# The first pair of tanh rows of the first chunk: by TensorE transposes and VectorE copies, or by a transposing transfer

## Chip, cores and metric

The kernel runs on one core of one Trainium2 chip. The metric is the device time of one execution in microseconds; several runs are made and their median is given. The engines are TensorE (PE, with PEld for its weight loads), VectorE (DVE), ScalarE (ACT), GpSimd (POOL) and SyncE (SP), which only issues transfers.

## The reference

A speech encoder's joint network with its gradients, forward and backward in one program, all in bf16. x is [2, 16000, 256]. Two convolutions over time (3 taps, stride 2, each followed by a gelu) make f of [2, 4000, 256], and then:

```
fe = f @ w_f                                  # [b, t, 256]
ge = g @ w_g                                  # [b, 8, 256]
j  = tanh(fe[:, :, None, :] + ge[:, None, :, :])   # [2, 4000, 8, 256]
out = j @ w_o                                 # [2, 4000, 8, 256]
```

Given grad_out of out's shape, it also returns the gradients of x, w1, w2, g, w_f, w_g and w_o. The one that the change touches is the gradient of w_o: the sum over b, t and u of j (as a column) times grad_out (as a row).

## The kernel before

The two sequences of 4000 steps of t are laid end to end (with 16 columns between them) and cut into 16 chunks of 512 columns (`CW`, the last of 336). In a chunk everything stands with the 256 features on partitions (two tiles of 128, `KT`) and time along the free dimension. The 8 values of u are taken in 4 pairs (`up`), two u each.

One pair of a chunk runs through these steps (`joint_units`):

- `tanh` (L415): ScalarE writes JT, the tanh of FE plus a bias from GE, four instructions of 128x512 for a pair.
- `gj` (L659), for each u: ScalarE squares JT into JSQ; TensorE multiplies grad_out's columns (GOT) with w_o (L672); VectorE makes NGZ from JSQ and that product (L676). Four NGZ for a pair. GpSimd adds the NGZ up (L696).
- `o_block` (L717): the output rows, 4 blocks of 128 time steps, matmuls with JT as the weights (L722), then a copy out of PSUM to OUT (L724). In the first chunk blocks 1 and 3 are copied by VectorE, the others by ScalarE.
- `gwo` (L753): the gradient of w_o, 16 matmuls per pair that add into one PSUM tile, GWO_ps (L761). It contracts over time, so it needs the tanh rows with time on partitions: JR, the transposed JT, and GO, grad_out's rows. `gwo` of a pair runs inside the next pair's `joint_units` (`prev_gwo`).

JR is made by `load_jr` (L698): one transposing transfer from SBUF to SBUF, issued on SyncE's queue (L703), for a whole pair: 128 partitions x 2048 values. It is called right behind the pair's `tanh`.

SyncE's queue issues in order. Besides JR it carries the transposing loads of grad_out (GOT, L174, three buffers) and of x (XC, L162), the plain loads of grad_out's rows (GO, L204, three buffers), and the rows of F (FR, L506).

All matmul results but GWO_ps go through one pool of 7 PSUM tiles (`ps_f32` and `ps_bf`, one tag). So a new matmul group can start when an earlier tile has been copied out. The transposes by TensorE that the kernel has already (`transposes`, L492, and the weights' at L845) use the same pool, an identity matrix as the second operand, and a copy out by VectorE or ScalarE (L498, L846).

Between a pair's steps, `weave` (L774) puts work of other chunks: after each step of the pair it advances a list of units (`parts`) by a ratio, 0.4 in the first chunk. In the first chunk (n = 0, the `else` at L880) there is no backward work of an earlier chunk; the list holds empty units, the second convolution of the next chunk (`conv2`, L370) and its FE (L394). `weave` also issues the gelu steps that were put off (`later`, `late`; L277, L282).

The order of instructions on each engine is made by the framework's scheduler from these calls, so it follows the code only roughly; semaphores are set by it as well.

Of the kernel before, what the change touches and what calls it, by code (L numbers as in the profile page):

```python
# [13 lines left out]
BF16 = mybir.dt.bfloat16  # L14
# [8 lines left out]
P = 128  # L23
KT = 2
# [8 lines left out]
def kernel(  # L33
# [22 lines left out]
    nc = tc.nc  # L56
# [7 lines left out]
    def geom(n):  # L64
        c0 = n * CW
        return c0, min(CW, L - c0)
# [23 lines left out]
    def blocks(w):  # L90
        return [(o, min(P, w - o)) for o in range(0, w, P)]
# [29 lines left out]
    jrp = pool("jrp", 3)  # L121
# [5 lines left out]
    def ps_f32():  # L127
        return psp.tile([P, 512], FP32, name="ps", tag="ps")

    def ps_bf():  # L130
        return psp.tile([P, 8, P], BF16, name="pst", tag="ps")


    ident = const.tile([P, P], BF16, name="ident")
# [16 lines left out]
    S = [dict() for _ in range(G)]  # L151
# [122 lines left out]
    def pump(k):  # L274
        for _ in range(k):
            if later:
                later.popleft()()  # L277
# [107 lines left out]
    def fe_units(n):  # L385
        c0, W = geom(n)
        if n > 0:
            pump(len(later))
        FE = fep.tile([P, KT, CW], FP32, name="FE")
        S[n]["FE"] = FE  # L390
        for mt in range(KT):
            ps = ps_f32()
            for kt in range(KT):
                nc.tensor.matmul(ps[:, :W], lhsT=WF[:, kt, mt * P:(mt + 1) * P], rhs=S[n]["FT"][:, kt, :W],  # L394
                                 start=(kt == 0), stop=(kt == KT - 1))
            nc.scalar.copy(out=FE[:, mt, :W], in_=ps[:, :W])
            yield
# [7 lines left out]
    def packed(ap, names, n, **kw):  # L405

        W = geom(n)[1]
        nb = -(-W // P)
        if nb * P == CW:
            return ap  # L410
        flat = ap.rearrange(f"p {names} -> p ({names})")
        size = flat.shape[1] // (CW // P) * nb
        return flat[:, :size].rearrange(f"p ({names}) -> p {names}", **kw)
# [245 lines left out]
    def gj(n, u):  # L659
        c0, W = geom(n)  # L660
        st = S[n]
        JT, GOT = st["JT", u], st["GOT", u]
        JSQ = jsp.tile([P, KT, CW], BF16, name="JSQ")
        jsq = nc.scalar.activation(out=JSQ[:, :, :W], in_=JT[:, :, :W], func=ACT.Square)  # L664
        if u == U - 4:
            st["JSQ"] = jsq
        NGZ = ngzp.tile([P, KT, CW], BF16, name="NGZ")
        st["NGZ", u] = NGZ
        for mt in range(KT):
            ps = ps_f32()  # L670
            for kt in range(KT):
                nc.tensor.matmul(ps[:, :W], lhsT=WOT[:, kt, mt * P:(mt + 1) * P], rhs=GOT[:, kt, :W],  # L672
                                 start=(kt == 0), stop=(kt == KT - 1))
            for b, lo, hi in spans(n):
                slot = n if b == 0 else n - segs_b1
                nc.vector.scalar_tensor_tensor(out=NGZ[:, mt, lo:hi], in0=JSQ[:, mt, lo:hi], scalar=1.0, in1=ps[:, lo:hi],  # L676
                                               op0=ALU.subtract, op1=ALU.mult,
                                               accum_out=NGGEc[:, b, mt, u, slot:slot + 1])
            yield
# [18 lines left out]
    def load_jr(n, up):  # L698

        W = geom(n)[1]  # L700
        JR = packed(jrp.tile([P, 2, KT, 4, P], BF16, name="JR")[:], "u k a d", n, u=2, k=KT, d=P)
        S[n]["JR", up] = JR
        S[n]["JRD", up] = nc.sync.dma_start_transpose(out=JR.rearrange("p u k a d -> p (u k a) d"),  # L703
                                    in_=S[n]["JTP", up].rearrange("p u k w -> p (u k w)"))

    def joint_units(n, up):
        c0, W = geom(n)
        st = S[n]
        bl = blocks(W)
        us = (2 * up, 2 * up + 1)  # L710
        for u in us:
            yield from gj(n, u)
            ngfe_acc(n, u)
        OUT = outp.tile([P, 4, 2 * V], BF16, name="OUT")
        JR = st["JR", up]

        def o_block(k):  # L717
            o, M = bl[k]
            ps = ps_f32()
            for j, u in enumerate(us):  # L720
                for kt in range(KT):
                    nc.tensor.matmul(ps[:M, j * V:(j + 1) * V], lhsT=st["JT", u][:, kt, o:o + M], rhs=WO[:, kt, :],  # L722
                                     start=(kt == 0), stop=(kt == KT - 1))
            (nc.vector.tensor_copy if n == 0 and k % 2 else nc.scalar.copy)(out=OUT[:M, k, :], in_=ps[:M, :])  # L724

        pend = prev_gwo[0]
        o_block(0)
        yield
        o_block(1)
        yield  # L730
        if pend is not None:
            gwo(*pend, 0)
        yield
        if pend is not None:
            gwo(*pend, 1)
        yield
        for k in range(2, len(bl)):
            o_block(k)
            yield
            if pend is not None:  # L740
                gwo(*pend, k)
        yield
        if pend is not None:
            for k in range(len(bl), len(blocks(geom(pend[0])[1]))):
                gwo(*pend, k)
        yield
        prev_gwo[0] = (n, up)
        for b, q, m, p0, p1, k, nb in joint_rows(n):
            nc.gpsimd.dma_start(out=joint_dram(out_0, b, q, m, up, nb), in_=OUT[p0:p1, k:k + nb, :])  # L749
# [3 lines left out]
    def gwo(n, up, k):  # L753
        bl = blocks(geom(n)[1])
        if k >= len(bl):
            return
        o, M = bl[k]
        JR, GO = S[n]["JR", up], S[n]["GO", up]
        for j in range(2):
            for dt in range(KT):  # L760
                nc.tensor.matmul(GWO_ps[:, dt, :], lhsT=JR[:M, j, dt, k, :], rhs=GO[:M, k, j * V:(j + 1) * V],  # L761
                                 start=(n_gwo[0] == 0), stop=(n_gwo[0] == last_gwo))
                n_gwo[0] += 1
# [6 lines left out]
    def empty(k):  # L770
        for _ in range(k):
            yield
# [88 lines left out]
        pass  # L861
    for u in range(2):
        tanh(0, u)
    load_jr(0, 0)

    for n in range(G):
        back, fwd = n > 0, n + 1 < G
        conv = conv_units(n + 1) if back and fwd else iter(())
        conv2 = conv2_units(n + 1) if fwd else iter(())
        late_open[0] = False  # L870
        parts = []
        if back:
            d1, e, rows, ghr = d1_units(n - 1), e_units(n - 1), row_units(n - 1), ghr_units(n - 1)
            parts += [islice(conv, 2), islice(d1, 1), islice(conv, 1), d1, conv, braid(rows, d5_units(n - 1)),
                      gwf_units(n - 1), gw2_units(n - 1), islice(ghr, 1), islice(conv2, 1), ghr, conv2, islice(e, 6)]
            if fwd:
                parts.append(fe_units(n + 1))
            parts.append(e)
        else:
            parts += [empty(6), islice(conv2, 1), empty(3), conv2, empty(6), fe_units(n + 1)]  # L880
        if not fwd:
            parts.insert(0, empty(2))
        fill = chain(*parts)
        ratio = (0.92 if n > 0 else 0.4) if n + 1 < G else 0.72
        for up in range(U // 2):
            step = n * (U // 2) + up
            if step + 2 < len(orderp):
                load_got(*orderp[step + 2])
            if step + 1 < len(orderp):
                load_go(*orderp[step + 1])  # L890
            if up == 3:
                load_fr(n)
            if back and up < 2 and n < G - 1:
                load_xr(n - 1, 2 * up)
                load_xr(n - 1, 2 * up + 1)
            if n == G - 2 and up >= 2:
                for piece in ((0,), (1, 2))[up - 2]:
                    load_xr_early(n, piece)
            main = joint_units(n, up)
            weave(main, fill, ratio)  # L900
            if up == U // 2 - 1:
                for _ in fill:
                    pump(2)
                    pump_late(1)
                pump(len(later))
                late_open[0] = True
                pump_late(len(late))
            for i in range(2):
                if 2 * step + 2 + i < len(order):
                    tanh(*order[2 * step + 2 + i])  # L910
            if step + 1 < len(orderp):
                load_jr(*orderp[step + 1])
            if n + 2 < G:
                load_x(n + 2, (((0,), (1,), (), ()) if n == 0 else ((), (0,), (1,), ()))[up])
    n = G - 1
# [75 lines left out]
```

## Time and profile before

| what | value |
|---|---|
| median of 3 runs | 826.83 us (825.32 to 827.06) |
| the profiled execution, its own time | 818.44 us |
| span of its instructions | 816.4 us |
| TensorE busy, matmuls | 794.3 us (97%) |
| VectorE busy | 624.7 us (77%) |
| ScalarE busy | 673.1 us (82%) |
| JR transfers | 64, landing 4.4 to 17.0 us after issue, median 8.8 |

Times in the profile count from the span's start. `L761` is line 761 of the kernel. A row of the timeline gives start, length, engine, line, operation, tiles as out<-in, and how many instructions were merged; in brackets stands how long the engine was idle before and what ended that. PE's rows overlap, since a matmul's start comes before the end of the one ahead of it. The granted clock is TensorE's, 1.00 being full speed.

### The profile page before, as it was taken

Reading aid. Unit: us, or ns where it says so; the run is one execution under the profiler, and the core shown is the slowest. Engines: PE = TensorE matmul, PEld = TensorE weight load, DVE = VectorE, ACT = ScalarE, POOL = GpSimd, SP = SyncE. Lnnn points to the kernel's source line nnn. Section 1 sums busy time; section 2 is a strip of 40 time slices with the busy share of each in tenths; the row PEclk is TensorE's granted clock in tenths of the full one; section 3 lists DMA queues with packets and bytes.
Section 4 is the critical chain, followed back from the end, with each engine's and each line's share of the span. In section 5 each row is a group of like instructions: output and inputs, shape, how many; then the busy total and the mean of one; then the engine's idle time right before and its main releaser. Section 6 shows DMA issues by size and latency. Waiting matters only on the chain.

```text
span 816.4 us, 16454 instructions
## 1 busy us (share of the span) xinstructions
PE 794.3 (97%) x6233; PEld 592.8 (73%) x6310; DVE 624.7 (77%) x1199; ACT 673.1 (82%) x1068; POOL 392.0 (48%) x418
## 2 busy tenths in 40 slices
PE   8788999999999999999999999999999999999998
PEld 3455877867777776777768778687786777778796
DVE  4988786977869778697886868778697786968744
ACT  5888897996979979799797978969799697987743
POOL 1364454553454535445476634535445355445641
PEclk9999999999999999999999999999999999999999
DMA  9999999999999999999999999999999999999954
GB/s 220 205 248 259 231 274 151 248 228 225 233 265 235 273 241 264 172 259 179 265 187 264 250 235 227 264 217 267 239 211 270 231 235 243 257 205 295 259 109 140
DMA packets 401423, 189.38 MB, mean 232 GB/s; under 512 B 349296, under 2 KB 385048, under 8 KB 401344
## 3 DMA queue, kind: packets, MB, share of 16 engines
q1 hardware_dynamic: 381104, 121.43, 83.0%
q0 software_dynamic: 20240, 66.89, 26.1%
q8 instruction: 49, 0.80, 0.4%
q14 instruction: 30, 0.25, 0.1%
HBM read 51.39 MB, written 50.34 MB: 125 GB/s over the span
## 4 chain that ended last, share of the span: by engine, by line
PE 86%; ACT 5%; DVE 4%; DMA 3%; issue 1%; POOL 0%; SPq 0%
PE GWO_ps L761 13%; PE ps L722 12%; PE ps L672 11%; PE ps L627 10%; PE ps L640 10%; PE ps L337 8%; PE ps L564 5%; PE pst L496 5%; PE ps L370 4%; PE ps L483 4%; PE ps L546 2%; DMA JR<-JT 2%; PE ps L460 1%; ACT JT L423 1%; PE ps L394 1%
## 5 line engine op out<-in xcount | busy, mean ns | idle before, releaser
L696 POOL TENSOR_TENSOR ACCN<-ACCN,NGZ 128x1024 f32<-128x1024 f32 (+1 forms) x80 | 168.3, 2104 | 69.2 <-DVE NGZ L676 68.4
L676 DVE SCALAR_TENSOR_TENSOR NGZ<-JSQ,ps 128x512 bf16<-128x512 bf16 (+3 forms) x272 | 168.2, 639 | 41.2 <-PE ps L672 33.3
L423 ACT ACTIVATE JT<-FE,GE 128x512 bf16<-128x512 f32 (+3 forms) x272 | 176.2, 711 | 0.5
L724 ACT CAST OUT<-ps 128x512 bf16<-128x512 f32 (+1 forms) x244 | 141.9, 596 | 32.0 <-PE ps L722 31.8
L664 ACT ACTIVATE JSQ<-JT 128x1024 bf16<-128x1024 bf16 (+1 forms) x128 | 135.1, 1058 | 35.8 <-DVE NGZ L676 35.6
L761 PE MATMUL GWO_ps<-GO,JR 128*128 128x256 bf16 (+1 forms) x1008 | 149.2, 274 | 5.8 <-DMA JR<-JT 4.8
L722 PE MATMUL ps<-WO,JT 128*128 128x256 bf16 (+1 forms) x1008 | 147.9, 273 | 0.1
L749 POOL DMA_DIRECT2D out_dram<-OUT x76 | 55.8, 734 | 170.1 <-ACT OUT L724 156.2
L672 PE MATMUL ps<-GOT,WOT 128*128 128x512 bf16 (+1 forms) x481 | 133.5, 376 | 1.4 <-DVE W2T L846 1.0
L761 PEld LDWEIGHTS <-JR 128*128 128x128 bf16 (+1 forms) x1008 | 97.4, 98 | 33.5 <-DMA JR<-JT 6.0
L722 PEld LDWEIGHTS <-JT 128*128 128x128 bf16 (+1 forms) x1008 | 97.5, 98 | 21.4 <-ACT JT L423 0.4
L627 PE MATMUL ps<-W1T,GH 128*128 128x256 bf16 (+2 forms) x756 | 100.2, 273 | 0.7
L277 DVE SCALAR_TENSOR_TENSOR g_s<-g_sq,g_x 128x1024 bf16<-128x1024 bf16 (+2 forms) x35 | 69.4, 1982 | 31.5 <-ACT g_sq L277 31.5
L627 PEld LDWEIGHTS <-GH 128*128 128x128 bf16 (+2 forms) x756 | 83.5, 116 | 13.0
L337 PE MATMUL ps<-XC,W 128*128 128x512 bf16 (+1 forms) x358 | 85.2, 374 | 3.0 <-DVE NGZ L676 1.8
L640 PE MATMUL ps<-rows,XR 128*128 128x256 bf16 (+1 forms) x708 | 84.7, 273 | 0.0
L630 ACT CAST GX<-ps 128x512 bf16<-128x512 f32 (+2 forms) x126 | 72.4, 589 | 12.1 <-PE ps L627 6.9
L444 DVE TENSOR_TENSOR ACC<-ACC,ps 128x512 f32<-128x512 f32 x84 | 57.5, 684 | 31.2 <-PE ps L564 24.8
L259 POOL DMA_DIRECT2D out_dram<-GX x66 | 36.2, 549 | 88.0 <-ACT GX L630 86.4
L640 PEld LDWEIGHTS <-XR 128*128 128x128 bf16 (+1 forms) x708 | 69.3, 98 | 11.0
L672 PEld LDWEIGHTS <-WOT 128*128 128x128 bf16 x512 | 48.4, 98 | 32.9 <-issue 2.4
L337 PEld LDWEIGHTS <-W 128*128 128x128 bf16 x384 | 37.4, 98 | 40.5 <-issue 3.0
(134 smaller groups left out, 1214.8 us busy)
## 6 DMA issues: line engine op xcount, KB each, us to landing
GO<-in_grad_out_dram SPq DMA_DIRECT2D x56, 512.0 KB, 5.8
out_dram<-OUT POOLq DMA_DIRECT2D x56, 512.0 KB, 6.1
out_dram<-GX POOLq DMA_DIRECT2D x55, 256.0 KB, 5.0
XR<-in_x_dram POOLq DMA_DIRECT2D x36, 256.0 KB, 6.8
XR<-in_x_dram POOLq DMA_DIRECT2D x12, 320.0 KB, 7.9
GO<-in_grad_out_dram SPq DMA_DIRECT2D x4, 384.0 KB, 5.9
out_dram<-OUT POOLq DMA_DIRECT2D x4, 384.0 KB, 5.6
GOT<-in_grad_out_dram SPq DMA_TRANSPOSE x68, 6.8
```

Source lines behind the costliest of these rows:

```text
L337: nc.tensor.matmul(ps[:, :W], lhsT=W1[:, i, kt, mt * P:(mt + 1) * P], rhs=st["X", c][:, kt, 16 + sh:16 + sh + W], start=(k == 0), stop=(k ...
L423: act = nc.scalar.activation(out=JT[:, mt, lo:hi], in_=S[n]["FE"][:, mt, lo:hi], func=ACT.Tanh, bias=GE[:, b, mt, u:u + 1], scale=1.0)
L627: nc.tensor.matmul(ps[:M, cj * D:(cj + 1) * D], lhsT=GH[:, par, kt, o:o + s * (M - 1) + 1:s], rhs=W1T[:, i, kt, :], start=(j == 0), stop=( ...
L630: nc.scalar.copy(out=t[:M, 2 * cp:2 * cp + 2, :], in_=ps[:M, :])
L640: nc.tensor.matmul(ps[:, dt * D:(dt + 1) * D], lhsT=x_row(4 * k + i + 2 * (1 - par))[:M, dt * P:(dt + 1) * P], rhs=t[:M, g + 2 * par:g + 2 ...
L664: jsq = nc.scalar.activation(out=JSQ[:, :, :W], in_=JT[:, :, :W], func=ACT.Square)
L672: nc.tensor.matmul(ps[:, :W], lhsT=WOT[:, kt, mt * P:(mt + 1) * P], rhs=GOT[:, kt, :W], start=(kt == 0), stop=(kt == KT - 1))
L676: nc.vector.scalar_tensor_tensor(out=NGZ[:, mt, lo:hi], in0=JSQ[:, mt, lo:hi], scalar=1.0, in1=ps[:, lo:hi], op0=ALU.subtract, op1=ALU.mul ...
L696: st["last"] = engine.tensor_tensor(out=out, in0=in0, in1=st["NGZ", u][:, :, :W], op=ALU.add)
L722: nc.tensor.matmul(ps[:M, j * V:(j + 1) * V], lhsT=st["JT", u][:, kt, o:o + M], rhs=WO[:, kt, :], start=(kt == 0), stop=(kt == KT - 1))
L724: (nc.vector.tensor_copy if n == 0 and k % 2 else nc.scalar.copy)(out=OUT[:M, k, :], in_=ps[:M, :])
L761: nc.tensor.matmul(GWO_ps[:, dt, :], lhsT=JR[:M, j, dt, k, :], rhs=GO[:M, k, j * V:(j + 1) * V], start=(n_gwo[0] == 0), stop=(n_gwo[0] == ...
```

## The change

Pair 0 of chunk 0 no longer calls `load_jr`. A generator, `turned_jr`, makes its JR instead: for each of the two u of the pair one PSUM tile, 8 transposes of 128x128 on TensorE into it, and one copy of 128x1024 into JR by VectorE. The generator is put at the head of the first chunk's list of fill units, where its two units take the place of two of the six empty ones. So it runs inside `joint_units` of pair 0, its first unit after about three steps of the pair and its second after about five. JR is used first in pair 1, by `gwo`. The other 63 pairs keep the transfer.

```
+    def turned_jr(n, up):
+
+        JR = jrp.tile([P, 2, KT, 4, P], BF16, name="JR")
+        S[n]["JR", up] = JR
+        for j in range(2):
+            ps = ps_bf()
+            for i in range(KT * 4):
+                nc.tensor.transpose(out=ps[:, i, :], in_=S[n]["JT", 2 * up + j][:, i // 4, i % 4 * P:(i % 4 + 1) * P],
+                                    identity=ident[:])
+            nc.vector.tensor_copy(out=JR[:, j].rearrange("p k a d -> p (k a) d"), in_=ps[:])
+            yield
+
     def joint_units(n, up):
...
-        JR = st["JR", up]
...
-    load_jr(0, 0)
+    turned0 = turned_jr(0, 0)
...
-            parts += [empty(6), islice(conv2, 1), empty(3), conv2, empty(6), fe_units(n + 1)]
+            parts += [turned0, empty(4), islice(conv2, 1), empty(3), conv2, empty(6), fe_units(n + 1)]
```

The line `JR = st["JR", up]` in `joint_units` was not used there.

## The prediction

> **What bounds the kernel now.** I read the page first: who is busy, and which chain of work ended last.
>
> ```profile
> span 816.4 us, 16454 instructions
> PE 794.3 (97%) x6233; PEld 592.8 (73%) x6310; DVE 624.7 (77%) x1199; ACT 673.1 (82%) x1068; POOL 392.0 (48%) x418
> PE 86%; ACT 5%; DVE 4%; DMA 3%; issue 1%; POOL 0%; SPq 0%
> ```
>
> TensorE (PE) works 794.3 of 816.4 us, so only its 22 us of idle time can be won. The table by stretches shows how little of that the change can reach.
>
> ```profile
> 32.40:35.40 3.00, 0.01 (x1) 0.00 (x0) 3.00 (x8) 3.00 (x5) 0.00 (x0) 1.00 0.99 222
> 35.40:39.70 4.30, 4.27 (x20) 2.61 (x21) 4.25 (x12) 2.57 (x4) 4.14 (x4) 0.60 0.59 132
> 39.70:45.80 6.10, 5.96 (x39) 3.56 (x38) 3.10 (x8) 4.90 (x8) 4.39 (x3) 1.00 1.13 307
> 45.80:47.60 1.80, 0.00 (x0) 0.00 (x1) 1.61 (x5) 1.80 (x4) 0.15 (x1) 1.00 1.14 378
> 47.60:55.00 7.40, 7.26 (x52) 4.92 (x53) 6.17 (x12) 6.03 (x9) 5.21 (x3) 1.00 1.08 167
> 55.00:70.00 15.00, 12.94 (x77) 7.34 (x77) 14.96 (x28) 12.86 (x21) 9.65 (x8) 1.00 1.10 271
> 100.00:800.00 700.00, 695.06 (x5541) 528.01 (x5609) 541.84 (x1024) 588.14 (x938) 348.54 (x367) 1.00 1.12 235
> ```
>
> The columns are the stretch, its length, busy us of PE, PEld, DVE, ACT, POOL, then the granted PE clock and the DMA share. From 100 to 800 us PE works 695.06 of 700: a head start gained before 100 us reaches the end, because nothing behind it has slack to absorb it. Three things matter before that: PE stands still for 3.00 us at 32.4; the clock is 0.60 in the 4.30 us behind that; PE stands still again for 1.80 us at 45.8. Note that VectorE (DVE) is full (3.00 of 3.00, 4.25 of 4.30) exactly where the change adds work to it.
>
> The chain that ended last names both holes, and the timeline of PE the first:
>
> ```profile
> 29.63 5.75 DMA JR<-JT
> 35.43 0.43 PE GWO_ps L761 x2
> 36.71 0.21 PE GWO_ps L761
> 36.92 0.85 PE ps L672 x2
> 37.77 2.12 PE GWO_ps L761 x13
> 39.89 0.49 PE ps L722 x5
> 40.38 7.17 DMA JR<-JT
> 47.60 1.05 PE GWO_ps L761 x8
> 48.65 1.32 PE ps L370 x6
> ```
>
> ```profile
> 31.39 1.03 PE L672 MATMUL ps<-GOT,WOT 128*128 128x512 bf16 x3
> 35.43 0.43 PE L761 MATMUL GWO_ps<-GO,JR 128*128 128x256 bf16 x2 [3.02 <-DMA JR<-JT]
> ```
>
> The first chunk's first JR (pair 0), issued at 29.63, lands 5.75 us later, and PE waits 3.02 us for it. That is the transfer the change removes. The second JR (pair 1) is issued at 40.38, lands 7.17 us later, and PE waits for it again. The order on an engine is not that of the code: pair 0's GWO_ps matmuls ran before pair 1's output matmuls (L722), which the code writes first. So the place of the new instructions is an assumption.
>
> **The transfer that goes.** The order of SyncE's queue:
>
> ```profile
> 29.63 4.00 SPq L703 DMA_TRANSPOSE JR<-JT  x1
> 33.73 5.38 SPq L174 DMA_TRANSPOSE GOT<-in_grad_out_dram  x2
> 39.92 0.37 SPq L204 DMA_DIRECT2D GO<-in_grad_out_dram  x1
> 40.38 4.61 SPq L703 DMA_TRANSPOSE JR<-JT  x1
> ```
>
> Issuing JR 0 holds the queue 4.00 us. Without it the two GOT transfers behind it may start up to 4 us sooner; the second still waits until pair 1's L672 matmuls have read its buffer. PE waited for no GOT in this stage, so I count their head start at nothing by itself. GO at 39.92 takes the buffer of GO 0, free only when pair 0's GWO_ps matmuls end (39.89 in the chain), and JR 1 at 40.38 queues right behind it. So the end of pair 0's GWO_ps matmuls sets when JR 1 starts, 0.49 us later.
>
> **The transposes that come.** Sixteen, in two groups of 8. The nearest rows are the weights' transposes of the same size, and the rows' transposes with their copy of 128x1024 out of PSUM:
>
> ```profile
> 23.21 0.83 PE L845 MATMUL pst<-ident,W 128*128 128x128 bf16 x12
> 71.82 0.68 DVE L498 COPY rows<-pst 128x1024 bf16<-128x1024 bf16 x1
> 72.42 0.69 DVE L277 TENSOR_TENSOR HT<-g_s,g_x 128x1024 bf16<-128x1024 bf16 x1
> ```
>
> Twelve take 0.83 us; with the last one's drain of 0.22 taken off, they are 0.055 us apart. 16 x 0.055 = 0.9 us of PE, which lies in the 3.02 us hole: 0 on the path. If that cover were gone, 0.9. One copy occupies VectorE for 0.60 us (71.82 to 72.42), two for 1.2, and VectorE has no gap there. Each group also takes one of the 7 PSUM tiles that all stages share until its copy is done. PE gets such tiles as VectorE and ScalarE empty them, so pair 0's later matmuls (output blocks, L722) may come some 0.5 us later, and ScalarE's copies of them with it. ScalarE has room for that:
>
> ```profile
> 40.36 0.58 ACT L724 CAST OUT<-ps 128x512 bf16<-128x512 f32 x1 [2.39 <-PE ps L722]
> ```
>
> It idles 2.39 us before this, so 0. The new waits: a group of transposes waits for its PSUM tile, and behind it on PE stand pair 0's last L672 and L722 matmuls; a copy waits for its transposes, and behind it on VectorE stand the fourth NGZ and HT, and behind those ScalarE's next squares. Transposes at 29 to 31 us are done before VectorE gets to the copies, so I count no wait there.
>
> **When JR 0 is ready now.** This decides, and it is read from VectorE's own order:
>
> ```profile
> 33.03 1.21 DVE L277 SCALAR_TENSOR_TENSOR g_s<-g_sq,g_x 128x1024 bf16<-128x1024 bf16 x1
> 34.17 0.68 DVE L277 TENSOR_TENSOR HT<-g_s,g_x 128x1024 bf16<-128x1024 bf16 x1
> 34.77 0.67 DVE L676 SCALAR_TENSOR_TENSOR NGZ<-JSQ,ps 128x512 bf16<-128x512 bf16 x1
> 35.50 0.69 DVE L277 TENSOR_TENSOR HT<-g_s,g_x 128x1024 bf16<-128x1024 bf16 x1
> 36.11 1.28 DVE L724 CAST OUT<-ps 128x512 bf16<-128x512 f32 x2
> 37.31 0.68 DVE L676 SCALAR_TENSOR_TENSOR NGZ<-JSQ,ps 128x512 bf16<-128x512 bf16 x1
> 39.13 0.68 DVE L676 SCALAR_TENSOR_TENSOR NGZ<-JSQ,ps 128x512 bf16<-128x512 bf16 x1
> 40.80 0.69 DVE L724 CAST OUT<-ps 128x512 bf16<-128x512 f32 x1 [0.98 <-PE ps L722]
> ```
>
> In the code the first copy comes behind pair 0's third NGZ (done at 33.03 here), the second behind pair 0's first output block, that is ahead of the two OUT copies at 36.11. With the first copy anywhere before 34.77, the fourth NGZ ends at 35.38 + 0.60 = 35.98, HT at about 36.6, and the second copy at about 37.2. The bounds: 34.2, if both copies directly follow the third NGZ (33.03 + 1.2); 38.4, if the second falls behind both OUT copies (37.2 + 1.2). I take 37.2, the code's order.
>
> So JR 0 comes later than before (37.2 against 35.38), and still I expect a gain, because of what PE does meanwhile. Before, half of pair 1's L672 matmuls stood behind the first two GWO_ps matmuls and ran after the hole, at the lowered clock. Now I expect them in the hole, (each 0.43 us of PE for its pair, as fast as VectorE frees PSUM tiles at 33.03 and 33.6: the last ends near 34.3), and the hole then runs only from about 34.3 to 37.2 and is followed by 16 GWO_ps matmuls alone. At full clock (1.05 us for 8 with a drain: 0.11 apart) they take 16 x 0.109 = 1.74 us and end at 37.24 + 1.74 = 38.98, where they ended at 39.89: **-0.9 us**.
>
> **The second term.** JR 1 is then issued at 38.98 + 0.49 = 39.47. Its 7.17 us had GO, the second GOT and an OUT store for company; JR 0 needed 5.75. Two transposing transfers are further ahead now, so I take 6.1, between them and nearer 5.75, and land JR 1 at 45.57 instead of 47.55: -2.0 together, **-1.1 us** of it from the landing. PE itself arrives at 38.98 + 5.9 = 44.9, so JR 1 is still last. Bounds of this term: 0 (7.17 stays) and -1.4 (5.75).
>
> Behind it, L370 at 48.65 feeds ScalarE and the VectorE stretch from 55 to 70, full with 14.96 of 15.00 and so moved as a whole. Sum: -2.0 us, from 818.44 us of the profiled execution (span 816.4 and 2.04 around it) to 816.4. The median of the runs shown, 826.83, lies 8.39 above that execution; I carry the difference over: **824.8 us**.
>
> **The rivals.** *A, VectorE takes it back* (no change). The 1.2 us delays everything on it behind the copies: the last NGZ ends at 40.95 instead of 39.74, and its next OUT copy, which came at 40.80 after a wait of 0.98, then cannot come before 40.95. If the chain behind runs over VectorE rather than over JR 1, the sum is +0.15 us: 827.0. For it: VectorE is full from 32.4 to 39.7 us and again from 55 to 70. Against: it is busy only 3.10 of 6.10 us from 39.7 to 45.8, so it can catch up before JR 1 lands.
>
> *B, the copy stands too far back and the clock falls* (slower). Place: the second copy behind the two OUT copies, done at 38.4. PE then idles from 34.3 to 38.4, 4.1 us. The hole of 3.02 us cost the clock (0.60 behind it: a GWO_ps matmul every 0.21 us instead of 0.11), the one of 1.80 did not (1.00). So the price is 16 x 0.21 = 3.4 us, the matmuls end at 41.8, and with JR 1's 7.17 unchanged the chain is +1.9: 828.7. It decides from a second copy ending at 36.5 on: at half clock that gives 39.9, as before. If the clock fell at my 37.2, the matmuls would end at 40.6, and with 6.1 for JR 1 the sum is -0.4, no change.
>
> The Trainium skill, "TensorE: Matmul & The Clock Gate" ("Why this matters for your kernels"), says that idle gaps of more than about 3 us put the clock back to half, and Part 4 that transposes do not count as busy for this gate. The first agrees with the two holes here; of the second no run here shows anything, and by it the transposes at the hole's edge would lengthen it for the gate and make B's price due in my own case.
>
> ```profile
> 35.37 0.71 ACT L423 ACTIVATE JT<-FE,GE 128x512 bf16<-128x512 f32 x1
> ```
>
> *C, JR 1 gets ahead in SyncE's queue* (faster still). If JR 1 is placed ahead of GO, it starts when pair 1's last tanh is done (36.1 before, 36.5 to 36.7 behind the first copy) and lands before PE gets there, even after 7.17 us: 43.9 at most. PE then starts JR 1's matmuls at 44.9 instead of 47.60: -2.7, 815.7, or 824.1 on the median. For it: the order is made anew. Against: before, JR 1 was placed behind GO. The most that can be won is both holes and the slow clock: 3.02 + 1.80 + (4.30 - 2.6, which is 16 x 0.109 + 4 x 0.21) less 0.9 for the transposes, 5.6 us: 821.2.
>
> That the change doesn't do what it says (the transfer still there, or the fill shifted) I see no room for: two fill units replace two of six empty ones.
>
> **How the numbers follow.** Forecast 33%, C 12%, A 30% (with the half clock at 37.2), B 25%. A measurement of this kernel can tell about 0.2%, 1.65 us. Faster by more: forecast and C, 45%. Within: A, 30%. Slower: B, 25%. The likeliest time is 824.8; its own range with C is 821.8 to 825.2. The range for 8 in 10 takes in most of B: 821.8 to 829.4.
>
> **What would show it.** Right: PE no longer waits for a JR transfer at 32 to 35 us; the second copy of JR 0 ends near 37.2, PE idles under 3 us before, the clock of the next 4 us is 1.00; the last GWO_ps matmul of pair 0 ends near 39.0; JR 1 is issued near 39.5 and lands near 45.6; from 100 us on everything is about 2 us earlier. Wrong: a clock well under 1 between 36 and 42 us and JR 1 issued after 41 (B); JR 1 lands sooner but VectorE's stretch from 55 to 70 starts where it did (A); JR 1 issued ahead of GO (C). My sum falls if the new order moves pair 1's output matmuls ahead of pair 0's GWO_ps matmuls.

## The result and the profile after

In one comparison of 22 runs each, the changed kernel took a median of 822.47 us (817.38 to 847.04) and the kernel before 826.32 us (819.11 to 840.12): 3.85 us less. The medians here and below are over all runs, while the ratios leave out the slow ones, which lie over 1.5% above the fastest run of the same kernel. The ratio is 0.9941, with a 95% interval of 0.9913 to 0.9969: 0.59% faster. The forecast was -2.0 us, or 0.24%. The profiled execution of the changed kernel took 817.38 us, with a span of 815.6 us. That is only 1.06 us less than the profiled execution of before (818.44). So most of the gain isn't in the two traces that one would lay side by side first. Executions of one and the same kernel scatter by 10 us and more in most sets of runs.

The page of the changed kernel, its totals and its chain of work:

```profile
span 815.6 us, 16487 instructions
PE 793.9 (97%) x6248; PEld 593.4 (73%) x6326; DVE 625.8 (77%) x1201; ACT 673.0 (83%) x1068; POOL 392.7 (48%) x418
PE 85%; ACT 4%; DMA 4%; DVE 4%; issue 1%; POOL 1%; SPq 0%; POOLq 0%; DVEq 0%
```

The same stretches as before (PE, PEld, DVE, ACT, POOL busy, then the granted clock, the DMA share and GB/s):

```profile
32.40:35.40 3.00, 1.78 (x8) 0.77 (x8) 3.00 (x7) 3.00 (x5) 0.00 (x0) 1.00 1.21 242
35.40:39.70 4.30, 3.27 (x22) 2.24 (x23) 4.30 (x10) 4.30 (x7) 2.98 (x3) 1.00 0.77 153
39.70:45.80 6.10, 6.10 (x45) 4.30 (x44) 6.02 (x17) 5.64 (x9) 5.98 (x5) 1.00 1.15 119
45.80:47.60 1.80, 1.75 (x12) 1.06 (x11) 0.00 (x0) 0.00 (x0) 1.72 (x2) 1.00 1.08 353
47.60:55.00 7.40, 6.02 (x46) 4.20 (x45) 7.30 (x12) 6.10 (x9) 2.85 (x2) 1.00 1.16 285
55.00:70.00 15.00, 10.97 (x59) 5.79 (x60) 15.00 (x28) 11.49 (x18) 8.68 (x8) 1.00 1.13 253
100.00:800.00 700.00, 695.18 (x5543) 528.19 (x5610) 541.74 (x1024) 588.14 (x938) 348.55 (x367) 1.00 1.10 235
```

The first hole of before is filled in part and the second whole (PE 1.78 of 3.00 in the place of 0.01, 1.75 of 1.80 in the place of 0.00), and in this execution the clock is 1.00 throughout. But PE has lost time in the last two stretches of the start: 6.02 of 7.40 in the place of 7.26, 10.97 of 15.00 in the place of 12.94. VectorE is full there. From 100 to 800 us nothing differs.

The timeline of PE shows what came in the place of the holes, and those of VectorE and ScalarE where the copies went and what they waited for:

```profile
29.52 0.61 PE L713 MATMUL pst<-ident,JT 128*128 128x128 bf16 x8
35.81 0.59 PE L672 MATMUL ps<-GOT,WOT 128*128 128x512 bf16 x2 [0.90 <-DVE JR L715]
36.24 0.38 PE L772 MATMUL GWO_ps<-GO,JR 128*128 128x256 bf16 x2
41.76 0.60 PE L772 MATMUL GWO_ps<-GO,JR 128*128 128x256 bf16 x4
44.79 1.04 PE L772 MATMUL GWO_ps<-GO,JR 128*128 128x256 bf16 x8
51.92 1.08 PE L733 MATMUL ps<-WO,JT 128*128 128x256 bf16 x8 [1.31 <-ACT g_x L373]
53.07 1.05 PE L772 MATMUL GWO_ps<-GO,JR 128*128 128x256 bf16 x8
58.91 1.02 PE L394 MATMUL ps<-FT,WF 128*128 128x512 bf16 x3 [3.05 <-DVE FT L277]
```

```profile
35.08 0.68 DVE L715 COPY JR<-pst 128x1024 bf16<-128x1024 bf16 x1
36.88 0.68 DVE L715 COPY JR<-pst 128x1024 bf16<-128x1024 bf16 x1
47.70 0.69 DVE L735 CAST OUT<-ps 128x512 bf16<-128x512 f32 x1 [1.98 <-DMA out_dram<-OUT]
56.86 2.00 DVE L277 TENSOR_TENSOR FT<-g_s,g_x 128x1024 bf16<-128x1024 bf16 x1
```

```profile
47.69 0.58 ACT L735 CAST OUT<-ps 128x512 bf16<-128x512 f32 x1 [2.34 <-DMA out_dram<-OUT]
51.30 0.57 ACT L373 CAST g_x<-ps 128x512 bf16<-128x512 f32 x1
```

SyncE's queue has another order than before:

```profile
31.34 3.06 SPq L174 DMA_TRANSPOSE GOT<-in_grad_out_dram  x1
36.47 1.77 SPq L703 DMA_TRANSPOSE JR<-JT  x1
38.29 3.89 SPq L162 DMA_TRANSPOSE XC<-in_x_dram  x1
42.28 5.20 SPq L174 DMA_TRANSPOSE GOT<-in_grad_out_dram  x1
47.57 3.02 SPq L703 DMA_TRANSPOSE JR<-JT  x1
```

JR 1 is issued at 36.47 us (40.38 before), ahead of the second GOT and of GO (50.69 us), which used to stand in front of it. Its matmuls start at 44.79 us in the place of 47.60, without a wait. That is rival C of the prediction. By pair 2 (53.07 against 54.44) half of these 2.81 us is gone, and when PE starts the GWO_ps matmuls of chunk 1's second pair (96.50 against 96.77) only 0.28 us is left. That last start is the measure used below: from there on these two executions run at a constant distance (0.28 us again at 396 and at 745 us), and others do unless a later stall disturbs them. The rest of the 0.8 us between the two spans comes behind 745 us.

### The profile page after: what moved, and what is told of

The parts are those of the page before. It is cut to its first block, busy times and chain, and to the rows that moved or that the text cites. A ratio compares the mean times of both kernels' runs of the same rounds, so it can differ in the third digit from the quotient of the medians.

```text
span 815.6 us, 16487 instructions
## 1 busy us (share of the span) xinstructions
PE 793.9 (97%) x6248; PEld 593.4 (73%) x6326; DVE 625.8 (77%) x1201; ACT 673.0 (83%) x1068; POOL 392.7 (48%) x418
## 4 chain that ended last, share of the span: by engine, by line
PE 85%; ACT 4%; DMA 4%; DVE 4%; issue 1%; POOL 1%; SPq 0%; POOLq 0%; DVEq 0%
PE GWO_ps L772 12%; PE ps L733 12%; PE ps L672 10%; PE ps L627 10%; PE ps L640 10%; PE ps L337 8%; PE pst L496 5%; PE ps L564 5%; PE ps L483 5%; PE ps L370 4%; PE ps L546 2%; ACT JT L423 2%; PE ps L460 1%; DMA XR<-in_x_dram 1%; PE ps L394 1%
## 5 line engine op out<-in xcount | busy, mean ns | idle before, releaser
L733 PE MATMUL ps<-WO,JT 128*128 128x256 bf16 (+1 forms) x1008 | 148.4, 272 | 2.6 <-ACT g_x L373 1.3
L733 PEld LDWEIGHTS <-JT 128*128 128x128 bf16 (+1 forms) x1008 | 97.5, 98 | 24.2 <-issue 3.2
L277 DVE SCALAR_TENSOR_TENSOR g_s<-g_sq,g_x 128x1024 bf16<-128x1024 bf16 (+2 forms) x35 | 67.5, 1930 | 32.0 <-ACT g_sq L277 32.0
```

## The experiments

Two questions: why did the 2.8 us not stay in the profiled executions, and where is the larger gain of the medians? Each run below is set against runs of the kernel before on the same chip. "Start" is the time at which PE starts the GWO_ps matmuls of chunk 1's second pair.

| kernel | median us (runs) | ratio to before | span us | JR 1's matmuls | start | VectorE idle 30 to 70 us |
|---|---|---|---|---|---|---|
| before | 826.32 (22) | | 816.4 | 47.60 | 96.77 | 4.51 |
| before_third | 825.98 (6) | 1.0015 [0.9973, 1.0057] | 819.1 | 48.43 | 97.65 | 4.77 |
| before_again | 825.19 (12) | 1.0009 [0.9972, 1.0046] | 821.0 | 49.72 | 101.49 | 7.17 |
| before_light | 824.48 (12) | 0.9988 [0.9955, 1.0020] | 822.5 | 51.31 | 102.92 | 10.53 |
| before_warm | 828.72 (12) | 1.0018 [0.9974, 1.0061] | 828.9 | 52.96 | 99.76 | 4.12 |
| before_warm2 | 823.16 (12) | 0.9967 [0.9928, 1.0007] | 825.6 | 52.65 | 99.45 | 4.69 |
| after | 822.47 (22) | 0.9941 [0.9913, 0.9969] | 815.6 | 44.79 | 96.50 | 1.98 |
| after_again | 821.24 (12) | 0.9957 [0.9911, 1.0004] | 817.0 | 44.75 | 97.79 | 2.62 |
| after_light | 818.78 (12) | 0.9958 [0.9924, 0.9993] | 827.2 | 45.90 | 98.61 | 2.29 |
| kept_transfer | 821.66 (12) | 0.9965 [0.9927, 1.0002] | 817.2 | 45.22 | 96.92 | 2.62 |
| order_only | 820.23 (12) | 0.9975 [0.9936, 1.0014] | 817.4 | 46.97 | 98.05 | 4.18 |
| order_again | 820.64 (6) | 0.9954 [0.9907, 1.0000] | 836.8 | 46.50 | 97.57 | 3.51 |
| late_jr1 | 820.79 (12) | 0.9967 [0.9930, 1.0005] | 825.2 | 49.72 | 96.41 | 0.03 |
| late_again | 820.19 (6) | 0.9944 [0.9900, 0.9988] | 819.5 | 50.73 | 97.51 | 0.03 |
| two_pairs | 819.24 (12) | 0.9964 [0.9933, 0.9995] | 818.0 | 46.36 | 97.30 | 0.03 |
| two_again | 823.42 (6) | 0.9962 [0.9906, 1.0018] | 831.1 | 46.32 | 97.27 | 0.03 |

The spans over 823 us hold stalls behind 340 us, told of below; their starts come before these.

### The changed kernel and the one before, once more

The same two kernels, unedited, under new names.

after_again: 

> The changed kernel, unaltered, run again beside the kernel before, to see what repeats. Theory Q (SyncE's queue): the second JR is issued ahead of GO and the second GOT, so pair 1's GWO_ps matmuls start near 44.8 us (before: 47.6), and the 0.6% seen over 22 runs is the price of the stages in front of 100 us in an ordinary execution: ratio 0.991 to 0.997. Theory C (chance): the two profiled executions differ by 0.8 us of span only, and the 0.6% comes from how the executions fell: ratio 0.998 to 1.002.

before_again: 

> The kernel before, unaltered, as a control against itself. In four kernels that differ from it only in the first 60 us, about half of the runs lay within 2 us of their fastest, and of its own runs 7 in 57. Theory B (before is really hit more often by late stalls): ratio 0.998 to 1.002 and again few runs within 2 us of the fastest. Theory M (what is run as the reference is timed longer): ratio 0.994 to 0.997, about half of the runs within 2 us of the fastest. Theory N (noise of sets of runs): ratio anywhere from 0.996 to 1.004.

before_third: 

> The kernel before once more, to see how its start spreads. Theory J (in an ordinary execution JR 1 lands late, PE stands 4 to 5 us and then runs at half clock for some 7 us, which starves VectorE): pair 1's GWO_ps matmuls start at 49 to 51 us and chunk 1's second pair 4 to 6 us later than in the first profile (96.8), as in the two profiles that followed; ratio 0.998 to 1.002. Rival F (the first profile was the ordinary case): again 96 to 98.

The changed kernel repeats within some 1.3 us: 821.24 us, start at 97.79 us. The kernel before doesn't. Its first profile had a start at 96.77 us, its second at 101.49 us, its third at 97.65 us. With before_light below, which has the same instructions up to its start (102.92 us), that is two early starts and two late ones. The text calls them the good and the bad mode; four profiles are too few to say that there are only these two. The execution profiled first, 818.44 us against a median of 826, was one of the better. Over all comparisons, 16 of 127 reference runs and none of the 18 runs of before_again and before_third came under 820.5 us; of the changed kernel's, 17 of 34.

The bad mode is read from before_again: SyncE's queue, then PE, then VectorE, then ScalarE.

```profile
39.70 5.42 SPq L703 DMA_TRANSPOSE JR<-JT  x1
```

```profile
49.72 1.89 PE L761 MATMUL GWO_ps<-GO,JR 128*128 128x256 bf16 x8 [5.00 <-DMA JR<-JT]
51.40 2.77 PE L370 MATMUL ps<-HT,W 128*128 128x512 bf16 x6
```

```profile
56.17 0.69 DVE L724 CAST OUT<-ps 128x512 bf16<-128x512 f32 x1 [6.29 <-PE ps L722]
```

```profile
54.21 0.59 ACT L373 CAST g_x<-ps 128x512 bf16<-128x512 f32 x1 [6.66 <-PE ps L370]
```

JR 1 is issued earlier than in the first profile (39.70 against 40.38), and lands later, some 10.0 us after issue in the place of 7.17. PE waits 5.00 us. Then 8 GWO_ps matmuls take 1.89 us where the first profile showed 1.05, and 6 matmuls of L370 take 2.77 in the place of 1.47. The work of VectorE and ScalarE hangs on these matmuls' results, so both run dry, for 6.29 and 6.66 us. The granted clock stands in the table by stretches of before_again, and for comparison that of before:

```profile
50.00:52.00 2.00, 2.00 (x10) 1.27 (x9) 0.00 (x0) 0.00 (x0) 1.86 (x1) 0.50 1.31 212
50.00:60.00 10.00, 10.00 (x56) 6.26 (x55) 3.83 (x8) 5.53 (x8) 2.63 (x2) 0.73 0.87 202
```

```profile
50.00:52.00 2.00, 2.00 (x19) 1.60 (x17) 0.82 (x2) 2.00 (x4) 2.00 (x1) 1.00 1.24 272
50.00:60.00 10.00, 9.47 (x67) 6.33 (x66) 8.77 (x18) 9.33 (x15) 5.93 (x4) 1.00 1.07 222
```

PE looks busier in the bad mode (10.00 of 10.00), and does less: 56 matmuls against 67. VectorE works 3.83 us of 10 in the place of 8.77.

The loss can be split. JR 1's matmuls start 2.12 us later than in the first profile (49.72 against 47.60). From there to pair 2's it takes 9.29 us (59.01) in the place of 6.84 (54.44): 2.45 us more. Together 4.57, and at chunk 1's second pair it is 4.72 (101.49 against 96.77). In before_light, also in the bad mode, it is 3.71 + 2.18 and at the end 6.15.

### The queue's order alone

The kernel before, with two order marks that put the second GOT and GO behind JR transfers, as the changed kernel has them. In the first 70 us the traces show VectorE, ScalarE and GpSimd in the order of before, and PE too as far as its records go; pair 0 keeps its transfer. The transfer of x that the program orders behind JR 1 moves forward with it.

```
...
+            if n == 1 and up == 0:
+                tc.add_manual_dep(dma.ins, S[0]["JRD", 1].ins.name, NOSYNC, reason="gradient behind tanh rows")
...
+            if n == 0 and up == 3:
+                tc.add_manual_dep(dma.ins, S[0]["JRD", 2].ins.name, NOSYNC, reason="rows behind tanh rows")
```

order_only: 

> The kernel before, with JR 0 still made by the transposing transfer, but SyncE's queue ordered as in the changed kernel: the first GOT of chunk 1 behind JR 1, the last GO of chunk 0 behind JR 2. All other engines keep the order of before. Theory Q (the queue's order is the gain): ratio 0.994 to 0.997, JR 1 issued near 37 and landed near 43 us, no wait for it at 45.8; PE's 3 us wait for JR 0 stays. Theory L (the latency of JR 0 and the slow clock behind it are the gain): 0.999 to 1.001. Theory T (one transposing transfer less for SyncE and the DMA engines is the gain): 0.999 to 1.001.

order_again: 

> The kernel before with JR 1 ahead of the second GOT and the last GO, once more. Theory J: it breaks the chain although JR 0 is still a transfer: no wait for JR 1, chunk 1's second pair at 96 to 99 us, ratio 0.993 to 0.998. Theory L (JR 0's latency is the cause): ratio 0.999 to 1.001 and 100 us or later.

PE and SyncE's queue in order_only:

```profile
36.77 0.39 PE L765 MATMUL GWO_ps<-GO,JR 128*128 128x256 bf16 x2 [3.93 <-DMA JR<-JT]
```

```profile
36.82 2.27 SPq L707 DMA_TRANSPOSE JR<-JT  x1
```

PE still waits 3.93 us for JR 0, the hole that the change was to remove. JR 1 leaves the queue at 36.82 us, and PE, which needs it at 46.97 us, never waits for it: a landing after 10 us, as in the bad mode, would have been in time as well. The starts are 98.05 and 97.57 us, among those of the changed kernel, and the medians, 820.23 and 820.64 us, are near its own. So in these runs the order alone keeps the bad mode away, without a single PE transpose. This isn't proof: the intervals of the ratios reach or pass 1, and two of four profiles without the order marks had an early start too.

### The transposes without the queue's order

The changed kernel, with JR 1 put back behind the second GOT and GO. Beside the queue, the order on PE, VectorE and ScalarE in the first chunk differs in places from the changed kernel's (JR 1's 16 matmuls, for instance, run in one go), so this isn't the queue's order alone undone.

```
...
+            if step == 1:
+                load_got(*orderp[4])
+                load_go(*orderp[3])
+                load_jr(0, 1)
+                for key in (("GOTD", 1, 0), ("GOD", 0, 3)):
+                    tc.add_manual_dep(S[0]["JRD", 1].ins, S[0][key].ins.name, NOSYNC, reason="tanh rows last")
```

late_jr1: 

> The changed kernel with JR 1 put back behind the second GOT and the last GO of chunk 0, as in the kernel before; pair 0 is still turned by PE. Theory Q: JR 1 issued after pair 0's last GWO_ps matmul (42.3 in the changed kernel, perhaps 39 to 43 here), landed after 46, PE waits for it, ratio 0.998 to 1.002. Theory L and theory T: 0.994.

late_again: 

> The changed kernel with JR 1 behind the second GOT and the last GO, once more. If it is JR 0 by PE that matters and not the queue's order, chunk 1's second pair stays at 96 to 98 us, ratio 0.993 to 0.998, with a wait for JR 1 that VectorE's own queue of work covers. If the order is all, it starts at 100 us or later and the ratio is 0.999 to 1.001.

late_jr1 on PE, and its table by stretches:

```profile
49.72 2.69 PE L773 MATMUL GWO_ps<-GO,JR 128*128 128x256 bf16 x16 [2.34 <-DMA JR<-JT]
```

```profile
50.00:60.00 10.00, 9.78 (x63) 6.67 (x62) 10.00 (x20) 4.33 (x7) 4.08 (x3) 0.83 1.01 215
```

JR 1's matmuls start at 49.72 us, as late as in before_again's bad mode though behind a wait of 2.34 us only, and a spell at half clock follows (0.50 from 51 to 54 us, 0.83 over the ten). Yet the start is 96.41 us, the earliest of all. VectorE is busy 10.00 of 10 us, and idle for 0.03 us from 30 to 70. So in this execution, with work queued on VectorE, neither JR 1's lateness nor the half clock shows in the start; in late_again, without half clock (1.00 from 30 to 70 us), it is 97.51. With either half of the change, the order in the queue or the transposes, the start lay at 96.41 to 98.05 us in two profiles each; with both, at 96.50 to 98.61. They don't add up, and none is clearly earlier than the good mode of before (96.77 and 97.65).

### The transfer's own load

The changed kernel, with the transposing transfer of pair 0 still issued, into a JR buffer that nobody reads. The engines' order is that of the changed kernel.

```
+    spare = jrp.tile([P, 2, KT, 4, P], BF16, name="JR")
+    nc.sync.dma_start_transpose(out=spare.rearrange("p u k a d -> p (u k a) d"), in_=S[0]["JTP", 0].rearrange("p u k w -> p (u k w)"))
```

kept_transfer: 

> The changed kernel with the transposing transfer of pair 0 issued all the same, into a JR buffer that nobody reads; PE, VectorE and ScalarE keep the changed kernel's order, and SyncE's queue too but for the one transfer more. Theory T (one transfer less is the gain): as before, 0.999 to 1.001, JR 1 issued about 4 us later than in the changed kernel. Theory Q: JR 1 is still ahead of GO, issued near 38.5 to 40 because of the 4 us of the extra issue, so half of the gain stays, 0.996 to 0.998. Theory L: all of it stays, 0.994.

```profile
30.69 3.84 SPq L876 DMA_TRANSPOSE JR<-JT  x1
```

The transfer holds the queue for 3.84 us again, and start (96.92) and median (821.66, against 821.24 of after_again beside it) stay. JR 1 leaves the queue only 0.60 us later (37.07 against 36.47), and not at 38.5 to 40 us as expected, since without the transfer the queue stood idle from 34.40 to 36.47. The time of one transposing transfer less on the queue shows no worth here.

### Less traffic

Both kernels without the stores of out_0 in the chunks 3, 5, 7 and so on, counted from 0; that part of the output is not written. It was to take late stalls away, so that the start shows better in the medians.

```
-        for b, q, m, p0, p1, k, nb in joint_rows(n):
+        for b, q, m, p0, p1, k, nb in joint_rows(n) if n < 2 or n % 2 == 0 else ():
```

before_light: 

> The kernel before without the stores of the joint's output in the odd chunks from the third on (that part of the output is not written); the instructions of PE, VectorE, ScalarE and SyncE's queue are unchanged. Theory S (what scatters the runs is the slack of the JR transfers behind 100 us: transfers run close to the limit, and where one falls behind, PE stalls): nearly all runs within 2 us of the fastest, ratio 0.988 to 0.993, JR landing 10 us and more before PE needs it throughout. Rival R (the scatter has nothing to do with the load of the DMA engines): the same scatter, ratio 0.998 to 1.002.

after_light: 

> The changed kernel with the same stores left out. Theory S: the scatter is gone here too, and what is left between this and the kernel before without those stores is the start alone, 0.3 to 1.5 us faster (0.1 to 0.2%). If the change gives 0.6% for a reason of its own, the two still lie 4 to 6 us apart.

The medians are 824.48 and 818.78 us, 5.7 us apart, with 1 and 9 of the 12 runs under 820.5. In the profiles the starts are 102.92 and 98.61, 4.3 us apart. The scatter that was to vanish stayed (expected ratio of before_light 0.988 to 0.993, measured 0.9988), so this late traffic isn't what holds the kernel before above 824. The difference of the two medians is near what the bad mode costs (4.7 and 6.15 us). The executions without a profile can't be put to a mode, though, and after_light's profiled one had a 5.3 us wait for XC between 340 and 420 us.

### The second pair as well

The changed kernel, with pair 1's JR by PE transposes too; the transfer of x that was ordered behind JR 1 is ordered behind JR 2.

```
...
-            parts += [turned0, empty(4), islice(conv2, 1), empty(3), conv2, empty(6), fe_units(n + 1)]
+            parts += [turned0, empty(4), turned_jr(0, 1), islice(conv2, 1), empty(1), conv2, empty(6), fe_units(n + 1)]
...
-            if step + 1 < len(orderp):
+            if step + 1 < len(orderp) and step:
                 load_jr(*orderp[step + 1])
```

two_pairs: 

> The changed kernel with the second pair turned by PE too, so that SyncE's queue has no JR in the first chunk before pair 2. Theory Q (the queue's order and load at the start): PE has no wait for JR 1, but 1.2 us more of VectorE's full stretch; start 0 to 2 us earlier than in the changed kernel, ratio 0.992 to 0.996. Theory V (VectorE is by now the limit of the first 70 us): nothing won or 1 us lost, 0.995 to 0.998.

two_again: 

> Both first pairs turned by PE, once more. Theory V (the first 70 us are VectorE's, and what counts is that it never runs dry): VectorE idle under 0.5 us between 30 and 70 us, chunk 1's second pair at 96 to 98 us, ratio 0.993 to 0.997, as the changed kernel or up to 1 us better. If one more JR by PE is worth as much as the first, 92 to 94 us and 0.988 to 0.991.

The starts are 97.30 and 97.27 us, within the changed kernel's 96.50 to 98.61. VectorE is idle for only 0.03 us from 30 to 70 us, so no wait of it is left to be won there. The medians, 819.24 and 823.42 us, enclose the changed kernel's; no gain is shown.

### The wait or the clock

What was open: in the bad mode, does the wait for JR 1 starve VectorE, or the half clock behind it? The kernel before, with 11 matmuls of 128x512 that nobody reads inside that wait.

```
...
+        if (n, up) == (0, 2):
+            ps = ps_f32()
+            for _ in range(11):
+                warm_mm = nc.tensor.matmul(ps[:], lhsT=ident[:], rhs=W1[:, 0].rearrange("p k d -> p (k d)"), start=True, stop=True)
+                tc.add_manual_dep(warm_mm.ins, st["after"].ins.name, NOSYNC, reason="warm")
+                st["after"] = warm_mm
...
+                if n_gwo[0] == 16:
+                    tc.add_manual_dep(mm.ins, S[0]["after"].ins.name, NOSYNC, reason="warm")
```

before_warm: 

> The kernel before with 11 matmuls of 128x512 that nobody reads, some 2.4 us, on PE right ahead of JR 1's first matmul. Theory (the half clock behind the wait starves VectorE): with the idle stretch cut by 2.4 us the clock stays over 0.6 from 48 to 56 us also where JR 1 lands late; PE starts chunk 1's second pair by 99.5 us, ratio 0.996 to 0.998 of the kernel before. Rival (the wait itself, whatever the clock): start of chunk 1's second pair still at 101 to 103 us where JR 1 lands after 49.5 us, ratio 0.999 to 1.002.

before_warm2: 

> The same kernel once more, for a second look at its start. Theory of the half clock: no clock under 0.6 from 48 to 56 us, chunk 1's second pair by 99.5 us, ratio 0.996 to 0.998. Rival, the wait itself: the pair at 101 to 103 us where JR 1 lands late, ratio 0.999 to 1.002.

before_warm on PE, on ScalarE, on VectorE, and its table by stretches; the row of before on ScalarE comes last:

```profile
48.10 2.54 PE L733 MATMUL ps<-W,ident 128*128 128x512 bf16 x11
52.96 1.05 PE L767 MATMUL GWO_ps<-GO,JR 128*128 128x256 bf16 x8 [2.32 <-DMA JR<-JT]
53.84 1.47 PE L370 MATMUL ps<-HT,W 128*128 128x512 bf16 x6
```

```profile
55.35 0.59 ACT L373 CAST g_x<-ps 128x512 bf16<-128x512 f32 x1 [2.09 <-PE ps L370]
```

```profile
52.52 2.34 DVE L282 TENSOR_SCALAR g_x<-g_s 128x1024 bf16<-128x1024 bf16 x1
56.71 0.68 DVE L724 CAST OUT<-ps 128x512 bf16<-128x512 f32 x1
```

```profile
50.00:60.00 10.00, 7.62 (x53) 5.07 (x53) 9.95 (x16) 7.56 (x11) 5.28 (x3) 1.00 1.17 217
```

```profile
49.99 0.58 ACT L373 CAST g_x<-ps 128x512 bf16<-128x512 f32 x1 [1.38 <-PE ps L370]
```

PE is held up as long as in before_again: 2.54 us of idle matmuls and 2.32 us of wait, 4.9 together. JR 1 lands even later, at 52.9 us. But the clock stays 1.00, 8 GWO_ps matmuls take 1.05 us and 6 of L370 take 1.47. From JR 1's first matmul to ScalarE's copy of g_x it takes 2.39 us (52.96 to 55.35), as in before (47.60 to 49.99), against 4.49 in before_again (49.72 to 54.21) and in before_light (51.31 to 55.80). So the half clock costs 2.1 us between JR 1's first matmul and g_x.

What this does to the start by way of VectorE is less clear. VectorE is full here (9.95 of 10), but its order is another than in the kernel before: from 52.52 to 56.71 us it runs gelu steps that stand behind the OUT copy in the kernel before. PE, 5.36 us behind the first profile at JR 1, is 2.99 behind at the start (99.76), so it makes up 2.4 us where before_again lost 2.6 more; before_warm2 has the same order on VectorE and shows the same, 5.05 and 2.68. How much of that is the clock and how much the order, these runs can't tell. The start also missed the expected bound of 99.5 in before_warm, by 0.26, and its ratio (1.0018) the expected 0.996 to 0.998; before_warm2 (99.45, 0.9967) met both. Both executions lost some 2 us at JR 0 as well (PE starts pair 0's matmuls at 37.90 and 37.28), and late stalls hide what the medians, 828.72 and 823.16, could tell.

### The late stalls

In before_warm, PE; in late_jr1, PE:

```profile
428.95 1.03 PE L767 MATMUL GWO_ps<-GO,JR 128*128 128x256 bf16 x4 [6.26 <-DMA JR<-JT]
```

```profile
766.91 0.59 PE L461 MATMUL ps<-NGFE,WFT 128*128 128x512 bf16 x1 [8.47 <-POOL NGFE L697]
```

The first costs before_warm some 9 us in all, the second late_jr1 9.7. Others stand in order_again (8.1 us for NGFE and 4.7 for GX, 740 to 790 us) and two_again (7.1 us for GOT, 600 to 720 us). They occur in kernels of both kinds and at different places, and each is larger than the whole effect of the change. Why they come in one execution and not in the next stays open.

## Why the prediction was partly right

- **The direction and the removed wait: right.** In the first chunk PE waits for no JR transfer, and the clock is 1.00 from 32.4 to 39.7 us.
- **VectorE's order: right.** The second copy occupies VectorE until 37.48 us (36.88 + 0.60); 37.2 was expected. The copies are 0.60 us each, and the transposes 0.056 us apart: 0.61 less the drain of 0.22, over 7.
- **"I count no wait there", for the PSUM tiles of the transposes: wrong.** PE stood 0.90 us at 35.81 and 0.57 us at 37.62 until the copies into JR had freed their tiles. As it had done other matmuls in the hole, it still reached JR 1's matmuls when the sum said.
- **"The matmuls end at 38.98": wrong, without a price.** Pair 1's output matmuls (L733) were mixed in among pair 0's GWO_ps matmuls, which end near 42.1 us (four from 41.76 on). The prediction named this as what would break its sum. It would have, had JR 1 still stood behind GO: in late_jr1, where it does, JR 1 left at 42.88 us.
- **"JR 1 is then issued at 39.47", the second term: wrong.** Rival C took place, at a chance of 12%: JR 1 left at 36.47 us, and its matmuls began at 44.79, where C said 44.9. The argument against C, that before JR 1 was placed behind GO, was none: the scheduler orders anew what the program's calls reorder.
- **That a head start stays: wrong in the profiled execution.** Of C's 2.81 us, 0.28 remains. The prediction said that VectorE's stretch from 55 to 70 us moves as a whole. What met the head start first was a store. OUT has two buffers, so pair 2's copies into it wait until pair 0's store (issued at 39.36 us) has landed: ScalarE stood 2.34 us and VectorE 1.98 us, until 47.7. ScalarE ran on without a gap from there to g_x, for which PE waited 1.31 us. VectorE was full from there on (7.30 of 7.40, 15.00 of 15.00) and finished FT at 58.8 us, for which PE waited 3.05 us and started L394 at 58.91, where the kernel before starts it without a wait:

```profile
57.07 1.03 PE L394 MATMUL ps<-FT,WF 128*128 128x512 bf16 x3
```

  The chain of after_again goes the same way:

```profile
39.31 7.74 DMA out_dram<-OUT
47.14 0.69 DVE OUT L735
56.90 1.93 DVE FT L277
58.87 0.58 PE ps L394
```

  The four profiles of the changed kernel's order (after, after_again, after_light, kept_transfer) all have both waits. In after_again and after_light the one for FT is 3.6 us long, and the clock is 0.50 from 60 to 64 us. It is rival A in another place: ScalarE and VectorE take the head start back, not at 40 us but from 46 us on. A third buffer for OUT was not tried.
- **"I carry the difference over" from the profiled execution to the median: the step that failed most.** The sum said -2.0 us for both; the profiled executions differ by 1.06 us and the medians by 3.85. The step took the 8.39 us between profiled execution and median as a constant of the kernel that the change leaves as it is. At least a part of it belongs to the place that the change touches. In two of four profiles of the kernel before and its lighter form, JR 1 lands 8.7 to 10 us after issue, PE waits 5 us, and the clock falls to half; that costs 4.7 and 6.15 us. In none of the ten profiles of kernels with the other order or the transposes does the 5 us wait occur, and none starts that late (96.41 to 98.61). The second term was mis-sized for the same reason: 7.17 us was one execution's landing, not the transfer's.

What stays open: the share of executions of before in the bad mode (four profiles are too few), hence how much of the 4 us is this mode. It can't be all that lifts the median: the two profiled executions in the bad mode took 822.96 and 824.27 us, still less than 826. Between the fastest runs of the two kernels (818.44 and 817.38 us) there is only 1.06 us. Open is also why the same transfer lands after 7.1 us or after 10.

## What to carry to other kernels

Ask first how far the profiled execution lies from the median, and whether a wait on the path is of a kind that varies, such as a transfer's landing: a change that removes the wait is worth its usual size, not the size in a lucky trace. Read the issue queue's order in the changed kernel before anything else, since taking one transfer out lets others pass, and here, in two profiles, order marks alone brought the same start. A head start on one engine only lasts until the next full engine or the next buffer that isn't free yet, so look for the engine that fills up and for the store that has to land.

## What the runs showed of the hardware

A wait of about 3 us can leave the clock alone or not. PE's wait for JR 0 in before_again and in before_third:

```profile
36.04 0.39 PE L761 MATMUL GWO_ps<-GO,JR 128*128 128x256 bf16 x2 [2.94 <-DMA JR<-JT]
```

```profile
36.40 0.39 PE L761 MATMUL GWO_ps<-GO,JR 128*128 128x256 bf16 x2 [3.42 <-DMA JR<-JT]
```

Behind 2.94 us the clock was 1.00 from 36 to 40 us; behind 3.42 us it was 0.85 from 36 to 38 us and 0.50 from 38 to 40, and behind the 3.02 us of the first profile 0.60 on average over the next 4.3 us. After 5.00 us (before_again) it was 0.50 from 49 to 55 us and back at 1.00 from 56, some 6 us after PE had work again; after 2.34 us of late_jr1, with a stretch of little work before, 0.50 from 51 to 54 and back by 55. The Trainium skill, "TensorE: Matmul & The Clock Gate" (Part 1), has a free-running window of about 3.4 us that decides on the clock. The rows agree with it in that the length alone doesn't decide: 2.94 us left the clock alone and 3.02 us didn't. A window that must be idle throughout doesn't fit the fall behind 2.34 us; how much work in it is too little, no run here shows. The half clock of before_again lasted about twice such a window.

The same transfer, JR 1 of the kernel before, was issued at 39.70 to 42.56 us and landed after 7.1 to 10.0 us in the four profiles of before, before_third, before_again and before_light, in an order of the queue that did not change.
